# Adaptive layer norm, 32-head attention and a gated feed-forward on one core: earlier weight parts, a wider choice of score bank, and other thresholds for VectorE's share of the softmax

## The chip, the cores and the metric

The kernel runs on one core of a Trainium2 chip. The metric is the device time of one execution in microseconds (us); the median of several executions is quoted. The first execution of the kernel before took 3633 us and is left out of every ratio. A profiled span is some 1.7 us shorter than the time of the same execution.

## The reference

`x` has 2048 tokens of width 512. There are 32 heads of 16, and the feed-forward is 1792 wide. All inputs are bfloat16.

```python
mod = (silu(c) @ w_mod).reshape(1, 6, 1, -1)          # sa, ca, ga, sb, cb, gb
h = layernorm(x) * (1 + ca) + sa
q, k, v = split_heads(h @ wqkv)                       # 32 heads of 16
p = softmax(q @ k.T / 4)                              # 32 x 2048 x 2048 probabilities
x = x + ga * (merge_heads(p @ v) @ wo)
h = layernorm(x) * (1 + cb) + sb
x = x + gb * ((gelu(h @ w_gate) * (h @ w_up)) @ w_down)
```

The 134 million exponentials of the softmax are the bulk of the elementwise work.

## The kernel before

The program is written by a scheduler that runs when the kernel is built. A recorder keeps, for each engine, a model of when it will be free, and a greedy loop picks the next instruction. What the chip gets are fixed streams, one for each engine, run in their order (the 1.22 us wait of VectorE at 742 us in after, below, shows it), with semaphore waits between them. So a constant that looks like a threshold changes the order of thousands of instructions.

Scores are made by TensorE in banks of 128 keys by 512 columns in PSUM. Two engines turn a bank into probabilities:

- ScalarE takes two or three banks in one exponential (1024 or 1536 columns).
- VectorE makes an approximate exponential for the four head positions of one round, a *quad*. It converts each of the four banks to 16-bit integers whose bits are a bfloat16 number (one conversion for each bank), and then writes four copies shifted by a constant (the *shift copies*). The product with V and the sum of the softmax are taken over all five versions, which smooths the approximation. A shift copy may also be done by GpSimd.

The constants that matter, and the place where a quad is started:

```python
AHEAD = 24      # a quad must lie at least so far ahead in the sequence of scores
WIDE = 0        # VectorE's bank may be the last bank of the other half (off)
PRESS = 6       # no new bank for a quad while a waiting quad's unit has so few plain rounds left
QA = 6          # quads only from this round of a unit on (and up to QB)
URGENT = 9      # a shift copy is urgent, and stays off GpSimd, below so many plain rounds
...
if len(mem) == CH and pos >= FIRST and not self.pressed() and self.free["dve"] + 600 < ...:
    while quad is None and cand and rounds[cand[0]][2] < pos + (... AHEAD):
        cand.pop(0)
    ...
self.act(self.E[:, e0:e0 + n, :], self.scp[:, s0:s0 + n, :], ACT.Exp, scale=EXP_SCALE)
...
self.ts("dve", kq[...].bitcast(U16), self.scp[:, gb, :], 128 / OCT, SHIFT_C, ALU.mult, ALU.add)
```

While attention for later tokens runs, the output projection and the feed-forward of earlier tokens are done as *side work* in one PSUM bank, `ps_mi`, and its weights are fetched in parts of 256 KB.

When TensorE would be idle for long, the scheduler puts in *filler* products, whose results nobody reads. They are meant to keep its clock up.

The softmax here doesn't subtract the row's maximum and nothing guards it: scores larger than these inputs give would overflow.

## Time and profile before

| | before |
|---|---|
| median time | 845.5 us (845.4 with one more execution; later sessions 844.6 to 844.9) |
| span of the profiled execution | 842.2 us |
| first attention exponential; end of the last one | 15.5 us; 815.6 us |
| ScalarE idle between these two | 4.2 us |
| score banks on ScalarE / VectorE (counted in the program) | 1704 / 344 |

The head of the profile's page shows the busy time of each engine and its share of the span, and the chain of work that ended last, by engine and by line.

```profile
span 842.2 us, 28224 instructions
PE 780.4 (93%) x12684; PEld 278.9 (33%) x12689; DVE 710.2 (84%) x1345; ACT 810.1 (96%) x747; POOL 117.7 (14%) x71
ACT 79%; PE 12%; DVE 4%; DMA 3%; SPq 1%; issue 0%; DVEq 0%
ACT E L364 76%; PE ps_mi L351 5%; PE ps_sc L351 5%; ACT wreg L364 3%; PE ps_pv L351 2%; DMA rb<-scr_rec 1%; DMA scr_rec<-rden 1%; SPq L415 1%; DVE mreg L376 1%; DVE wreg L381 0%; DMA xs<-in_A_x_dram 0%; DMA mreg<-in_B_w_down_dram 0%; DVE st L404 0%; DVE wreg L368 0%; DVE dreg L376 0%
```

ScalarE is busy for 96% of the span, and three quarters of the chain are its exponentials. TensorE is busy for 93% too, but part of that is filler.

These are the groups of instructions by form on ScalarE. The columns are: line, engine, operation, tiles and shapes, count | busy us, mean ns of one | idle us before it and what ended most of that.

```profile
L364 ACT ACTIVATE E<-ps_sc 128x1536 bf16<-128x1536 f32 x320 | 453.7, 1538 | 3.1 <-PE ps_sc L351 2.8
L364 ACT ACTIVATE E<-ps_sc 128x1024 bf16<-128x1024 f32 x372 | 366.0, 1133 | 1.5 <-PE ps_sc L351 1.4
```

And the largest groups of VectorE's conversions and of the shift copies on VectorE and GpSimd (the others write or read the tile `mreg`; in all there are 344 conversions, and 284 + 60 copies):

```profile
L376 DVE TENSOR_SCALAR dreg<-ps_sc 128x512 uint16<-128x512 f32 x228 | 153.9, 685 | 21.3 <-PE ps_sc L351 19.6
L376 DVE TENSOR_SCALAR mreg<-dreg 128x2048 uint16<-128x2048 uint16 x185 | 119.6, 683 | 3.1 <-PE ps_pv L351 2.8
L376 POOL TENSOR_SCALAR mreg<-dreg 128x2048 uint16<-128x2048 uint16 x43 | 81.5, 1898 | 309.3 <-DVE mreg L376 92.3
```

A mean times a count is more than the busy time on ScalarE (1538 ns x 320 is 492 us), because the instructions overlap. What one exponential costs in a full queue is its spacing. In a row of three 1536-wide ones (4.13 us in all, where a lone one took 1.45 us), that is (4.13 - 1.45) / 2 = 1.34 us.

Busy time by windows, with the columns busy us (and count) for PE, PEld, DVE, ACT and POOL, then the granted TensorE clock, the DMA share and GB/s:

```profile
117.00:640.00 523.00, 492.41 (x6910) 149.56 (x6911) 481.59 (x844) 521.54 (x484) 108.02 (x57) 1.00 0.14 39
640.00:806.00 166.00, 150.49 (x3335) 66.83 (x3332) 107.34 (x216) 164.60 (x137) 0.00 (x0) 1.00 0.38 108
```

In the 523 us of the middle ScalarE is busy for 521.5 and VectorE for 481.6. VectorE has real room in the last stage only, where it is busy for 107 of 166 us.

### The profile page before, as it was taken

What the parts mean: (1) busy time and instruction counts of PE and PEld (TensorE: products, weight loads), DVE (VectorE), ACT (ScalarE), POOL (GpSimd) and SP (SyncE); (2) the same over time, 40 slices, a digit from 0 to 9 for tenths busy, and PEclk for the clock granted to TensorE, in tenths of its full rate; (3) what the DMA queues carried; (4) which work ended last, traced back from release to release, by engine and by line L of the source; (5) the groups of instructions that cost most, each with busy time, mean ns of one, the idle gap of its engine ahead of it and who ended that gap; (6) DMA issues with size and microseconds to landing.
All of it is one profiled execution on the core that took longest, in us unless ns stands there. A gap on an engine that the chain in (4) does not pass through costs nothing.

```text
span 842.2 us, 28224 instructions
## 1 busy us (share of the span) xinstructions
PE 780.4 (93%) x12684; PEld 278.9 (33%) x12689; DVE 710.2 (84%) x1345; ACT 810.1 (96%) x747; POOL 117.7 (14%) x71
## 2 busy tenths in 40 slices
PE   8899999999999998989999999899998998988997
PEld 3333333322222222222222222222343333335556
DVE  7878899899899999999889999999887886376484
ACT  5999999999999999999999999999999999999982
POOL 1000102031220331142210130333000000000000
PEclk9999999999999999999999999999999999999999
DMA  9000000000003111111003111111013222185330
GB/s 315 13 27 17 16 15 15 17 15 15 15 16 90 44 36 52 52 41 46 16 28 96 52 53 32 48 40 40 27 25 103 78 72 65 37 235 158 92 96 14
DMA packets 74931, 47.68 MB, mean 57 GB/s; under 512 B 17693, under 2 KB 70618, under 8 KB 74810
## 3 DMA queue, kind: packets, MB, share of 16 engines
q1 hardware_dynamic: 72426, 44.30, 18.1%
q8 instruction: 99, 1.62, 0.8%
q10 hardware_dynamic: 2384, 1.57, 0.7%
q14 instruction: 22, 0.18, 0.1%
HBM read 43.25 MB, written 2.61 MB: 54 GB/s over the span
## 4 chain that ended last, share of the span: by engine, by line
ACT 79%; PE 12%; DVE 4%; DMA 3%; SPq 1%; issue 0%; DVEq 0%
ACT E L364 76%; PE ps_mi L351 5%; PE ps_sc L351 5%; ACT wreg L364 3%; PE ps_pv L351 2%; DMA rb<-scr_rec 1%; DMA scr_rec<-rden 1%; SPq L415 1%; DVE mreg L376 1%; DVE wreg L381 0%; DMA xs<-in_A_x_dram 0%; DMA mreg<-in_B_w_down_dram 0%; DVE st L404 0%; DVE wreg L368 0%; DVE dreg L376 0%
## 5 line engine op out<-in xcount | busy, mean ns | idle before, releaser
L364 ACT ACTIVATE E<-ps_sc 128x1024 bf16<-128x1024 f32 (+2 forms) x700 | 782.7, 1311 | 17.4 <-PE ps_sc L351 16.9
L351 PE MATMUL ps_sc<-qT,kmo 32*128 32x512 bf16 (+2 forms) x1408 | 171.9, 323 | 10.5 <-ACT E L364 9.3
L351 PE MATMUL ps_sc<-qT,kme 32*128 32x512 bf16 (+2 forms) x1344 | 162.1, 331 | 18.2 <-ACT E L364 16.5
L376 DVE TENSOR_SCALAR dreg<-ps_sc 128x512 uint16<-128x512 f32 x228 | 153.9, 685 | 21.3 <-PE ps_sc L351 19.6
L351 PE MATMUL ps_pv<-E,vaug 128*17 128x512 bf16 (+2 forms) x2308 | 157.1, 321 | 1.3 <-DVE vaug L385 0.8
L351 PE MATMUL ps_pv<-mreg,vaug 128*17 128x512 bf16 (+2 forms) x1644 | 129.1, 354 | 4.1 <-DVE mreg L376 3.1
L376 POOL TENSOR_SCALAR mreg<-dreg 128x2048 uint16<-128x2048 uint16 x43 | 81.5, 1898 | 309.3 <-DVE mreg L376 92.3
L351 PE MATMUL ps_mi<-wreg,mreg 128*32 128x512 bf16 (+1 forms) x1792 | 113.7, 355 | 10.2 <-DVE wreg L381 5.5
L376 DVE TENSOR_SCALAR mreg<-dreg 128x2048 uint16<-128x2048 uint16 x185 | 119.6, 683 | 3.1 <-PE ps_pv L351 2.8
L351 PEld LDWEIGHTS ps_sc<-qT,kme 32*128 32x128 bf16 x1344 | 42.8, 91 | 146.5 <-ACT E L364 123.0
L376 DVE TENSOR_SCALAR mreg<-ps_sc 128x512 uint16<-128x512 f32 x116 | 78.5, 685 | 14.9 <-PE ps_sc L351 13.8
L351 PEld LDWEIGHTS ps_sc<-qT,kmo 32*128 32x128 bf16 x1408 | 46.4, 91 | 128.0 <-ACT E L364 101.7
L351 PEld LDWEIGHTS ps_pv<-E,vaug 128*17 128x17 bf16 x2308 | 47.6, 89 | 62.9 <-issue 50.8
L376 DVE TENSOR_SCALAR mreg<-mreg 128x2048 uint16<-128x2048 uint16 x99 | 65.1, 686 | 3.0 <-PE ps_pv L351 2.5
L351 PEld LDWEIGHTS ps_mi<-wreg,mreg 128*32 128x32 bf16 x1792 | 39.4, 95 | 57.4 <-issue 18.9
L351 PEld LDWEIGHTS ps_pv<-mreg,vaug 128*17 128x17 bf16 x1644 | 37.5, 88 | 51.0 <-DVE mreg L376 24.5
L385 DVE CAST wreg<-ps_mi 128x512 bf16<-128x512 f32 x49 | 33.6, 687 | 15.9 <-PE ps_mi L351 15.6
L376 POOL TENSOR_SCALAR mreg<-mreg 128x2048 uint16<-128x2048 uint16 x17 | 32.3, 1897 | 93.8 <-DVE onorm L368 23.0
L381 DVE SCALAR_TENSOR_TENSOR wreg<-wreg,ps_mi 128x512 bf16<-128x512 bf16 x49 | 33.4, 682 | 12.8 <-PE ps_mi L351 5.6
L351 PE MATMUL ps_mi<-hreg,wreg 128*32 128x512 bf16 x480 | 39.5, 384 | 0.5 <-DVE qT L376 0.5
L351 PE MATMUL ps_mi<-wo,onorm 128*32 128x512 bf16 x480 | 36.6, 382 | 0.1
L368 DVE TENSOR_TENSOR wreg<-wreg 128x1024 bf16<-128x1024 bf16 (+1 forms) x56 | 34.1, 618 | 0.5
(138 smaller groups left out, 597.8 us busy)
## 6 DMA issues: line engine op xcount, KB each, us to landing
mreg<-in_B_w_up_dram SPq DMA_DIRECT2D x32, 256.0 KB, 3.1
mreg<-in_B_w_gate_dram SPq DMA_DIRECT2D x28, 256.0 KB, 2.9
rb<-scr_rec SPq DMA_DIRECT2D x96, 64.0 KB, 2.0
mreg<-in_B_w_down_dram SPq DMA_DIRECT2D x16, 256.0 KB, 2.8
dreg<-in_B_w_down_dram SPq DMA_DIRECT2D x12, 256.0 KB, 4.0
mreg<-in_w_mod_dram SPq DMA_DIRECT2D x1, 2048.0 KB, 14.4
out_dram<-xs SPq DMA_DIRECT2D x16, 128.0 KB, 1.8
rb<-scr_rec SPq DMA_DIRECT2D x52, 32.0 KB, 2.6
```

The source lines that it names most:

```text
L351: return self.rec("pe", lambda e: e.matmul(out, lhsT, rhs, start=start, stop=stop, tile_position=tp), [lhsT, rhs], [out], cost=(n, int(rhs ...
L364: return self.rec("act", lambda e: e.activation(out, in_, func, scale=scale, **kw), rd, wr, cost=self.cost("act", out, [in_], "act"))
L368: return self.rec(eng, lambda e: e.tensor_tensor(out, a, b, op), [a, b], [out], cost=self.cost(eng, out, [a, b], "tt"))
L376: return self.rec(eng, lambda e: e.tensor_scalar(out, a, s1, s2, **kw), rd, [out], cost=self.cost(eng, out, [a], "ts"))
L381: return self.rec("dve", lambda e: e.scalar_tensor_tensor(out, a, s, b, op0=op0, op1=op1), rd, [out], cost=self.cost("dve", out, [a, b], " ...
L385: return self.rec(eng, lambda e: e.tensor_copy(out, in_), [in_], [out], cost=self.cost(eng, out, [in_], "ts"))
L415: return e.dma_start(out, in_)
```

## The change

Its intent in a few words: weight parts of the feed-forward are fetched two chunks ahead; VectorE's score bank may take the free side bank; shift copies turn urgent later, and quads come sooner. The diff, cut to its core:

```diff
-AHEAD = 24
+AHEAD = 20
-WIDE = 0
-PRESS = 6
+SIDE = 1024
+PRESS = 5
-QA = 6
+QA = 5
-URGENT = 9
+URGENT = 6
 ...
         def load(x, ci):
-            if flow and ci < len(chunks):
+            if flow and ci < len(chunks) and not self.dry:
 ...                              (the fetch becomes a task of the SP queue)
-            load(0, 0)
-            load(1, 0)
+            for i in range(2):
+                load(0, i)
+                load(1, i)
 ...                              (G and U: load(x, ci + 1) before the chunk's products becomes)
+                if b0 + kpb >= m:
+                    load(0, ci + 2)          # after them; likewise load(1, ci + 2)
 ...
-                        if n == CH and (s0 or not WIDE or pos < nsplit + 12
-                                        or self.probe(lambda: self.mm(self.scp[:, SC - 1, 0:P], *filler)) > t + 30):
+                        if n == CH and (self.open or self.credit > SIDE
+                                        or self.probe(lambda: self.mm(self.mi[:, 0:P], *filler)) > t + 30):
                             continue
 ...
                     if n == CH:
-                        gb = SC - 1
+                        gb = self.mi[:, :]
```

With the side bank, VectorE's bank needs no place among the score banks, so ScalarE's exponential keeps all three of its banks.

More of the change, by code (lines that the diff above doesn't have):

```diff
@@ L946, in load @@
         def load(x, ci):
-            if flow and ci < len(chunks):
+            if flow and ci < len(chunks) and not self.dry:
                 v = (self.B_w_gate, self.B_w_up)[x].rearrange("(a p) n -> p a n", p=P)
-                self.dma("sp", self.wst[x][ci % 2], v[:, :, 2 * P * ci:2 * P * ci + 2 * P], "st%d%d" % (x, ci % 2))
+                self.task([("sp", lambda: self.dma("sp", self.wst[x][ci % 2], v[:, :, 2 * P * ci:2 * P * ci + 2 * P],
+                                                   "st%d%d" % (x, ci % 2)))], None)
         def load_down(i):
@@ L979, in G @@
             g, w = self.gw[:, ci % 2, 0, 0:m * W], self.gw[:, ci % 2, 1, 0:m * W]
-            load(0, ci + 1)
             for b0 in range(0, m, kpb):
@@ L996, in U @@
             yield from self.until(("gelu", gi, ci))
-            load(1, ci + 1)
             for b0 in range(0, m, kpb):
@@ L1001, in U @@
                 yield from up(1, ci, sub)
+                if b0 + kpb >= m:
+                    load(1, ci + 2)
                 self.stt(w[:, W * b0:W * (b0 + k)], w[:, W * b0:W * (b0 + k)], 1.0, mi[:, 0:W * k], ALU.add, ALU.mult)
@@ L1349, in stream @@
                         mem, after = take(CH)
-                gb = s0 + CH - 1
+                gb = self.scp[:, s0 + CH - 1, :]
                 if g is not None:
                     for n in (CH, CH - 1):
-                        if n == CH and (s0 or not WIDE or pos < nsplit + 12
-                                        or self.probe(lambda: self.mm(self.scp[:, SC - 1, 0:P], *filler)) > t + 30):
+                        if n == CH and (self.open or self.credit > SIDE
+                                        or self.probe(lambda: self.mm(self.mi[:, 0:P], *filler)) > t + 30):
                             continue
@@ L1364, in stream @@
                     g += j
-                items = [(m, s0 + i) for i, m in enumerate(mem)]
+                items = [(m, self.scp[:, s0 + i, :]) for i, m in enumerate(mem)]
                 if g is not None:
@@ L1381, in stream @@
                         pass
-                    self.ts("dve", kq[:, 512 * j:512 * j + 512].bitcast(U16), self.scp[:, gb, :], 128 / OCT, SHIFT_C,
+                    self.ts("dve", kq[:, 512 * j:512 * j + 512].bitcast(U16), gb, 128 / OCT, SHIFT_C,
                             ALU.mult, ALU.add)
@@ L1436, in qk @@
         for kk in range(max(512 // it[0][0][3] for it in items)):
-            for ((_, qd, q0, W), r, j), k in items:
+            for ((_, qd, q0, W), r, j), bank in items:
                 kpb = 512 // W
@@ L1442, in qk @@
                 dc, ee = qd // 2, qd % 2
-                self.mm(self.scp[:, k, W * kk:W * kk + W],
+                self.mm(bank[:, W * kk:W * kk + W],
                         self.km[ee][32 * j:32 * j + 32, dc, P * kt:P * kt + P],
```

## The prediction

> **What bounds the kernel.** Page: span 842.2 us, timed median 845.5. ScalarE is busy 810.1 us, 782.7 of it in softmax exponentials; the chain that ended last is 76% those. Busy time by windows: ScalarE is idle about 15 us before the first exponential, 1.8 in 15:117, 1.5 in 117:660, 1.4 in 660:817 and 19 in the tail after 817. Between 15 and 817 us the time is the number of score banks that ScalarE must exponentiate. VectorE takes the other banks (a 685 ns conversion each, then four 685 ns shift copies per quad of four banks, or 1.9 us each on GpSimd) and is 92% busy in 117:660, 65% in 660:817. TensorE is 93% busy, part of it fillers. Waits on weight transfers: some 3 us on TensorE, none on ScalarE, so fetching two chunks ahead removes little.
>
> **What the change moves** (instructions of both programs, counted in order):
> - VectorE takes 376 score banks instead of 344: 8 more quads. ScalarE: 1536-wide exponentials 320 to 291, 1024-wide 372 to 399, one more 512-wide. The free side bank is used only 5 times; most of the gain is quad timing.
> - Shifts: VectorE 284 to 269, GpSimd 60 to 107 (203 us instead of 114). VectorE net: about +12 us, all after 640 us, where it has room.
> - TensorE: 8 quads add 12 sets of four 512-wide and 40 sets of 256-wide products (at 0.22 and 0.11 us: 7 us); 27 filler sets fewer (6 us). About level.
> - Transfers keep their number.
>
> **Costing.** Instruction durations overlap on ScalarE (1311 ns times 700 is more than the busy time). Solving the busy sum with 427 ns per further bank, an estimate, gives 1.354 us per 1536-wide and 0.93 us per 1024-wide exponential. Saved: 29 x 1.354 - 27 x 0.93 - 0.49 = 13.7 us, nearly all critical: 5 us before 270 us, 3 in the middle, 5 in the last part. [...]the trace's two mean durations differ by 405.
>
> **What leaks.** TensorE has less slack per exponential, so ScalarE gets 1 to 4 us of new waits, mainly in the last part. Prologue and tail stay. [...]in the trace before one VectorE shift took 1155 ns instead of 685. With 107 shifts there, I expect a few more such stalls, 1 us in effect.
>
> **Prediction:** 833.5 us (1.4% faster), 829 to 841 in 8 of 10. Faster by over 2%: 0.13; within 2%: 0.86; slower: 0.01.
>
> **Signs.** Right: ScalarE busy near 796 us and over 98% between 20 and 800 us; GpSimd near 205 us; VectorE near 720; tail about 25 us; weight waits under 3 us. Wrong: ScalarE idle over 6 us in the middle, waiting on score matmuls (TensorE or VectorE became the bound); VectorE shifts often over 1 us[...]; a longer tail because the last feed-forward isn't done.
>
> **What would make it wrong.** The schedule is fixed by a model at build time; if the real machine drifts from it where GpSimd and VectorE interleave twice as densely, in-order queues lose the gain (toward 841). If the earlier weights also remove small stalls, over 2%.

The forecast's sum is 845.5 - 13.7 = 831.8 us, and 1.7 us of leak, out of the 1 to 4 named, make 833.5. The 427 ns had not been taken from a trace, but the traces show it: lone exponentials of 512, 1024 and 1536 columns took 597, 1023 and 1450 ns in before, so 426 and 427 ns a bank. They also show the two costs: the three- and two-bank exponentials are busy for 778.3 us in before (320 and 372 of them) and for 764.1 us in after (291 and 399), and the two sums together give 1.354 and 0.928 us. For the products, 4, 8 and 12 of 512 columns took 0.39, 0.60 and 0.82 us in before (near 341 us), and 8 and 32 of 256 columns 0.40 and 1.06 us in after (near 750 us): 0.22 and 0.11 us for a further set of four.

## More of the kernel before

In the last 100 us the remaining feed-forward weights are made resident, one part for every three positions of the score sequence:

```python
if parts and pos >= loaded and ("ffn", 2 if early else 3) in self.have:
    parts.pop(0)()
    loaded = pos + 3
```

## The result and the profile after

The kernel after takes 834.7 us in the median of four executions (832.6 to 836.2), against 845.4 before. The ratio is 0.9872, with a 95% interval of 0.9846 to 0.9899; a second session gave 834.6 us and 0.9871. Here and below a ratio is the mean time of one kernel's fast runs over that of the other's of the same rounds, so it is not quite the ratio of the medians. By the threshold of 2% this counts as the same, though it is clear of noise.

The head of the page after:

```profile
span 833.0 us, 28525 instructions
PE 779.5 (94%) x12784; PEld 280.8 (34%) x12789; DVE 722.4 (87%) x1362; ACT 797.2 (96%) x746; POOL 206.7 (25%) x118
ACT 77%; PE 12%; DVE 5%; DMA 3%; SPq 1%; issue 1%; POOL 0%; DVEq 0%
ACT E L364 75%; PE ps_sc L351 5%; PE ps_mi L351 5%; ACT wreg L364 2%; PE ps_pv L351 2%; DMA scr_rec<-rden 1%; DMA mreg<-in_w_mod_dram 1%; DMA rb<-scr_rec 1%; DVE wreg L381 1%; SPq L415 1%; DVE dreg L376 1%; POOL mreg L376 0%; DMA den<-scr_den 0%; DVE wreg L385 0%; DVE mreg L376 0%
```

ScalarE lost 13.0 us of busy time. VectorE gained 12 us and GpSimd 89 us, and TensorE's busy time did not change. The groups on ScalarE, then those of VectorE and GpSimd:

```profile
L364 ACT ACTIVATE E<-ps_sc 128x1536 bf16<-128x1536 f32 x291 | 413.4, 1527 | 5.4 <-PE ps_sc L351 5.3
L364 ACT ACTIVATE E<-ps_sc 128x1024 bf16<-128x1024 f32 x399 | 389.5, 1101 | 1.6 <-PE ps_sc L351 1.1
```

```profile
L376 DVE TENSOR_SCALAR dreg<-ps_sc 128x512 uint16<-128x512 f32 x246 | 166.3, 686 | 25.4 <-PE ps_sc L351 22.7
L376 DVE TENSOR_SCALAR mreg<-dreg 128x2048 uint16<-128x2048 uint16 x178 | 115.6, 683 | 1.0 <-PE ps_pv L351 0.9
L376 POOL TENSOR_SCALAR mreg<-dreg 128x2048 uint16<-128x2048 uint16 x70 | 132.8, 1901 | 278.7 <-DVE mreg L376 137.2
```

There are 29 fewer three-bank and 27 more two-bank exponentials. In all, 1672 banks are left to ScalarE before the tail, and 376 go to VectorE. The windows are the same as before:

```profile
117.00:640.00 523.00, 497.19 (x7089) 151.61 (x7087) 481.36 (x841) 522.52 (x488) 178.29 (x94) 1.00 0.15 41
640.00:806.00 166.00, 152.76 (x3544) 71.28 (x3540) 128.61 (x265) 162.02 (x139) 1.90 (x1) 0.99 0.37 105
```

In the middle nothing is lost: ScalarE is busy for 522.5 of 523 us, and VectorE does as much as before, because GpSimd took shift copies over. In the last stage ScalarE is idle for 4 us instead of 1.4.

It helps to cut each profiled span into three parts. *Attention work* is the time from the first exponential to the table load after the last one, less ScalarE's waits in it. The *rest* is everything else: the prologue, those waits and the tail. Before: 795.9 + 46.3. After: 783.0 + 50.0. So the work fell by 12.9 us and 3.7 us came back. Of these 3.7 us, 1.4 are in the prologue (the first exponential at 16.95 instead of 15.53 us; a second profile of the same kernel had 15.70, so this is not a property of the kernel: TensorE's granted clock was 0.50 from 11.7 to 15.1 us in the one execution, and 1.00 in the other and in before), and 2.1 are new waits in the net. After 720 us before has waits of 1.2 us. These are ScalarE's waits after, between 720 and 806 us:

```profile
ACT E L364 <- PE ps_sc L351: 3.9, 4, 1.7
```

And this is that place in the timelines of VectorE, then TensorE, then ScalarE, of the kernel after (start us, duration us, engine, line, operation, tiles, count; in brackets the idle time just before it and what ended it):

```profile
743.26 0.43 DVE L368 TENSOR_TENSOR onorm<-osb,rb 128x256 bf16<-128x256 f32 x1 [1.22 <-DMA rb<-scr_rec]
743.61 0.73 DVE L376 TENSOR_SCALAR hreg<-xs,mv,rstd 128x512 bf16<-128x512 bf16 x2
```

```profile
744.07 0.66 PE L355 MATMUL ps_mi<-ident,hreg 128*128 128x128 bf16 x4 [1.47 <-DVE hreg L376]
744.67 0.39 PE L351 MATMUL ps_sc<-qT,kme 32*128 32x256 bf16 x6
...
746.10 1.04 PE L351 MATMUL ps_sc<-xs,ident 128*32 128x512 bf16 x8
747.07 0.61 PE L351 MATMUL ps_sc<-qT,kme 32*128 32x256 bf16 x6
```

```profile
745.11 1.45 ACT L364 ACTIVATE E<-ps_sc 128x1536 bf16<-128x1536 f32 x1 [0.81 <-PE ps_sc L351]
747.73 2.92 ACT L364 ACTIVATE E<-ps_sc 128x1536 bf16<-128x1536 f32 x2 [1.17 <-PE ps_sc L351]
752.31 2.87 ACT L364 ACTIVATE E<-ps_sc 128x1536 bf16<-128x1536 f32 x2 [1.67 <-PE ps_sc L351]
```

Read it as a chain. At 742 us the next instruction in VectorE's queue is a normalisation that needs `rb`, the reciprocals of the softmax sums, which come back through memory; they land 1.22 us late. Behind it in the queue stands the instruction that makes `hreg`, which needs nothing of that sort. TensorE has a transpose of `hreg` next in its own queue and stands for 1.47 us, and no filler runs in the gap (TensorE is busy for 0.00 us between 742.64 and 744.07 us), because they too stand behind it. Shortly after this gap TensorE gets slow: the same six score products of 256 columns take 0.39 us at 744.67 and 0.61 us at 747.07, as the granted clock is down, to 0.50 from 745.6 to 749.0 us (such a stretch is called a *dip* below). Until 750.9 us it waits another 1.19 us, for a weight part. ScalarE waits three times, for 3.65 us. Only the second of these waits, of 1.17 us, lies in the dip: the first is over before it, and the third begins after it, at the wait for the weight part.

### The profile page after: what moved, and what is told of

Read it like the earlier page. It is cut to its first block, busy times and chain, and to the rows that moved or that the text cites. A ratio compares the mean times of both kernels' runs of the same rounds, so it can differ in the third digit from the quotient of the medians.

```text
span 833.0 us, 28525 instructions
## 1 busy us (share of the span) xinstructions
PE 779.5 (94%) x12784; PEld 280.8 (34%) x12789; DVE 722.4 (87%) x1362; ACT 797.2 (96%) x746; POOL 206.7 (25%) x118
## 4 chain that ended last, share of the span: by engine, by line
ACT 77%; PE 12%; DVE 5%; DMA 3%; SPq 1%; issue 1%; POOL 0%; DVEq 0%
ACT E L364 75%; PE ps_sc L351 5%; PE ps_mi L351 5%; ACT wreg L364 2%; PE ps_pv L351 2%; DMA scr_rec<-rden 1%; DMA mreg<-in_w_mod_dram 1%; DMA rb<-scr_rec 1%; DVE wreg L381 1%; SPq L415 1%; DVE dreg L376 1%; POOL mreg L376 0%; DMA den<-scr_den 0%; DVE wreg L385 0%; DVE mreg L376 0%
## 5 line engine op out<-in xcount | busy, mean ns | idle before, releaser
L364 ACT ACTIVATE E<-ps_sc 128x1024 bf16<-128x1024 f32 (+2 forms) x699 | 769.2, 1272 | 20.6 <-PE ps_sc L351 19.9
L376 POOL TENSOR_SCALAR mreg<-dreg 128x2048 uint16<-128x2048 uint16 x70 | 132.8, 1901 | 278.7 <-DVE mreg L376 137.2
L376 DVE TENSOR_SCALAR dreg<-ps_sc 128x512 uint16<-128x512 f32 x246 | 166.3, 686 | 25.4 <-PE ps_sc L351 22.7
L351 PE MATMUL ps_sc<-qT,kmo 32*128 32x512 bf16 (+2 forms) x1405 | 166.0, 323 | 10.7 <-ACT E L364 9.1
L351 PE MATMUL ps_pv<-mreg,vaug 128*17 128x512 bf16 (+2 forms) x1896 | 140.9, 346 | 2.0 <-DVE mreg L376 1.0
L351 PE MATMUL ps_mi<-wreg,mreg 128*32 128x512 bf16 (+1 forms) x1792 | 116.4, 356 | 10.2 <-DVE wreg L381 4.8
L376 POOL TENSOR_SCALAR mreg<-mreg 128x2048 uint16<-128x2048 uint16 x37 | 70.2, 1901 | 158.5 <-PE ps_sc L351 56.6
L376 DVE TENSOR_SCALAR mreg<-ps_sc 128x512 uint16<-128x512 f32 x125 | 84.9, 687 | 17.0 <-PE ps_sc L351 16.5
L351 PEld LDWEIGHTS ps_pv<-mreg,vaug 128*17 128x17 bf16 x1896 | 43.7, 89 | 49.6 <-DVE mreg L376 17.1
L376 DVE TENSOR_SCALAR mreg<-mreg 128x2048 uint16<-128x2048 uint16 x91 | 59.2, 685 | 0.2
L351 PEld LDWEIGHTS ps_mi<-wreg,mreg 128*32 128x32 bf16 x1792 | 38.8, 95 | 56.8 <-issue 20.3
L351 PE MATMUL ps_mi<-mreg,hreg 128*32 128x512 bf16 x448 | 38.1, 384 | 0.0
```

The lines of the kernel that those rows point to most:

```text
L351: return self.rec("pe", lambda e: e.matmul(out, lhsT, rhs, start=start, stop=stop, tile_position=tp), [lhsT, rhs], [out], cost=(n, int(rhs ...
L364: return self.rec("act", lambda e: e.activation(out, in_, func, scale=scale, **kw), rd, wr, cost=self.cost("act", out, [in_], "act"))
L376: return self.rec(eng, lambda e: e.tensor_scalar(out, a, s1, s2, **kw), rd, [out], cost=self.cost(eng, out, [a], "ts"))
```

## The experiments

Theory 1: the time follows what is left to ScalarE. Its rivals at first were theory 2 (the gain comes from shift copies moved to GpSimd) and theory 3 (it comes from weights that arrive earlier). Later came theory 4 (what is lost again is lost to late transfers in the last 100 us) and theory 5 (TensorE has simply too little time left per exponential there). In each experiment, what the scheduler made of the edit was counted in the built program before the run.

### One part of the change alone

Each starts from the kernel before (the side bank is never used).

load_only: only the weight parts two chunks ahead, with the old constants.

```diff
-            load(0, 0)
-            load(1, 0)
+            for i in range(2):
+                load(0, i)
+                load(1, i)
 ...                              (and the other hunks of load)
```

> The kernel before with only the weight parts fetched two chunks ahead. Counted in the program: VectorE takes 352 score banks (344 before, 376 after), GpSimd 60 shift copies as before. Theory 1 (the time follows what ScalarE has left to exponentiate; estimate 1.354 us per 1536-wide, 0.93 per 1024-wide exponential): 3.4 us less than before, about 842.0 us. Theory 2 (the gain comes from moving shift copies to GpSimd): no gain, about 845.4. Theory 3 (the gain comes from weights that arrive earlier, so TensorE waits less): most of the 10.7 us, 838 or less.

Measured: 848.7 us, ratio 1.0043 (1.0014 to 1.0073). It is slower than before. Theory 3 falls. Theory 1's number is missed by 6.7 us.

urgent_only:

```diff
-URGENT = 9
+URGENT = 6
```

> The kernel before with only URGENT 9 to 6, so that shift copies go to GpSimd more often: 112 of them instead of 60, VectorE 236 instead of 284, but only 348 score banks on VectorE (344 before). Theory 1: 1.7 us less than before, about 843.7 us, although VectorE is relieved of about 30 us of work. Theory 2: most of the gain, about 836 to 838. Theory 3: no gain.

Measured: 848.0 us, ratio 1.0037 (1.0011 to 1.0064). VectorE's busy time fell by 20 us, to 690.3, and GpSimd's rose to 216.3, and nothing was gained. Theory 2 falls. Theory 1's number is missed here too, by 4.3 us.

quads_only:

```diff
-AHEAD = 24
-PRESS = 6
-QA = 6
+AHEAD = 20
+PRESS = 5
+QA = 5
```

> The kernel before with only the quad timing (AHEAD 24 to 20, PRESS 6 to 5, QA 6 to 5): 356 score banks on VectorE, 67 shifts on GpSimd, 289 on VectorE. Theory 1: 5.1 us less than before, about 840.3 us, if VectorE, which now has 12 conversions and 5 shifts more, does not hold anything up. Theory 2 and 3: about 845; a loss, if VectorE at over 90% busy is what limits.

Measured: 847.7 us, ratio 1.0029 (1.0007 to 1.0050). Theory 1's number is missed by 7.3 us here. So theory 1 expected each of the three parts to be faster than before, and each was a little slower.

### The change without one part

no_side: the kernel after, with the side bank out of reach.

```diff
-SIDE = 1024
+SIDE = -1000000
```

> The kernel after without the free side bank (never taken): 356 score banks on VectorE, 105 shifts on GpSimd, weights two chunks ahead. After takes the side bank only 5 times. Theory 1: the other 20 banks that are lost with it count, so 8.6 us slower than after, 840 to 843 us. If only the direct use counted, 5 banks of 0.43 us: 2 us slower, about 837. Theory 2 and 3: about as fast as after, 835 to 837.

Measured: 845.5 us, ratio 1.0002 (0.9979 to 1.0025). The whole gain is gone with a bank that is used five times. Theory 1 named 840 to 843, so it is missed by 2.5 us, but in the right direction. Counting direct uses would have given 837.

old_load: the kernel after, with weight parts one chunk ahead as before.

```diff
-            for i in range(2):
-                load(0, i)
-                load(1, i)
+            load(0, 0)
+            load(1, 0)
 ...                              (and the other hunks of load)
```

> The kernel after with the weight parts fetched one chunk ahead, as before. Counted: 372 score banks on VectorE (376 in after), ScalarE 295 / 395 / 7. Theory 1: 1.7 us slower than after, 836 to 837 us. Theory 3 (earlier weights are what gives the gain): 840 or more. If the two chunks fetched at once crowd the transfers, as theory 4 allows, it could be as fast as after.

Measured: 835.0 us, ratio 0.9887 (0.9873 to 0.9902), 0.15 points behind after, or 1.3 us, in another session. That is about the one quad by which the programs differ, but the intervals overlap.

pool0: the kernel after, without GpSimd.

```diff
-POOLED = 1
+POOLED = 0
```

> The kernel after with no shift copies on GpSimd at all. Counted: the schedule then finds room for only 348 score banks on VectorE (376 in after), 348 shifts on VectorE, ScalarE 321 / 368 / 7. Theory 1: ScalarE's work as in before but for 1.8 us, so 843 to 846 us; GpSimd does not gain time by itself (urgent_only) but is needed to fit the quads. If GpSimd's shifts cost more than they bring[...], it would be below 840.

Measured: 843.2 us, ratio 0.9976 (0.9959 to 0.9993), as theory 1 said. With VectorE alone the scheduler finds room for 348 banks only. GpSimd is needed for the gain, but does not give it by itself.

### How far the other engines are behind ScalarE

narrow480 and narrow480_before: the two kernels with shorter exponentials. The order and number of all instructions stay the same (but for one fill of the columns left out), because the scheduler is still told the old cost.

```diff
-self.act(self.E[:, e0:e0 + n, :], self.scp[:, s0:s0 + n, :], ACT.Exp, scale=EXP_SCALE)
+ew, sw = self.E[:, e0:e0 + n, 0:480], self.scp[:, s0:s0 + n, 0:480]
+self.rec("act", lambda e, ew=ew, sw=sw: e.activation(ew, sw, ACT.Exp, scale=EXP_SCALE), [sw], [ew],
+         cost=self.cost("act", self.E[:, e0:e0 + n, :], [sw], "act"))
 ...
+self.memset(pool, self.E[:, 1:, 480:512], 1.0)
```

> The kernel after with each exponential of a score bank over 480 of its 512 columns; the other columns hold ones, so the result is wrong on purpose. Order and number of all instructions are as in after. ScalarE saves 1671 banks x 32 columns x 0.833 ns = 44.5 us (estimate). If ScalarE alone limits, about 790 us. If the other engines are close behind, as I expect with TensorE at 94% and VectorE at 92% busy, the time falls by 10 to 25 us, to 810 to 825, and ScalarE waits for score products all along: then further quads are worth less and less.

> The kernel before with each exponential of a score bank over 480 of 512 columns (wrong on purpose, order of all instructions as in before). ScalarE saves about 45 us of work (estimate: 1704 banks x 32 columns x 0.833 ns). In after the same cut gave only 9.5 us: there the other engines are that close behind. If the change used up a margin that before still had, this falls by clearly more, 16 to 22 us, to 823 to 829 us, near the same floor as after with the cut. If before had no more margin than after, it falls by about 10, to 835.

The 0.833 ns a column in both is what the traces of before and after show: a lone exponential of 512 columns took 597 ns, one of 1536 columns 1450 ns, and (1450 - 597) / 1024 = 0.833.

Measured: 825.2 us for after with the cut, ratio to before 0.9771 (0.9756 to 0.9786), and 835.1 us for before with the cut, 0.9882 (0.9863 to 0.9900). (Their outputs are wrong, which doesn't matter for the times. The comparison with the reference still passed, so its tolerance does not see this, and these are not valid kernels.) By that cost ScalarE is given 44.5 and 45.4 us less to do, and the time falls by 9.5 and by 9.8 us, just under the 10 to 25 us expected for narrow480. ScalarE's busy time falls by 28.7 and 30.0 us only, because its exponentials overlap less now (a mean of 1379 ns for 1440 columns, where it was 1527 and 1538 ns for 1536; in after, count times mean of the three-bank ones was 31 us above their busy time, with the cut 16 us). The second of the two expectations for narrow480_before holds: no margin was used up. The chain that ended last shows what took over, first in after with the cut, then in before with the cut:

```profile
PE 58%; DVE 25%; ACT 8%; DMA 3%; POOL 2%; issue 2%; SPq 1%; DVEq 0%; POOLq 0%
```

```profile
PE 50%; DVE 28%; ACT 13%; DMA 3%; issue 2%; POOL 2%; SPq 2%; DVEq 0%; POOLq 0%
```

ScalarE's share of the chain is down from 77% to 8%; TensorE and VectorE hold it. So in both kernels ScalarE sets the pace, but in this order of instructions only some 10 us, or 1.2%, ahead of the others. The order was laid out for the longer exponentials; whether one laid out for the shorter ones would be faster was not tried. This floor (the time with the cut) fell with the change, from 835 to 825 us. Which part of the rearrangement lowered it, the runs do not tell: TensorE's busy time is 784.0 and 779.6 us in the two.

### The leak

spread6 and spread5: the kernel after, with the resident weight parts further apart.

```diff
-                    loaded = pos + 3
+                    loaded = pos + 6          # spread5: pos + 5
```

> The kernel after, with the 21 transfers of the last feed-forward's resident weights issued every 6 positions of the score sequence instead of every 3. Counted: exponentials, conversions and shifts are exactly those of after (291 / 399 / 7, 376, 269 + 107); only the order within the last 100 us differs. Theory 4 (the leak of after, 3.9 us of ScalarE waiting between 737 and 754 us, comes from small transfers and weight parts that land late in a crowded transfer queue, and hold up the in-order queues of VectorE and TensorE): these waits go, 831 to 832 us. Theory 5 (TensorE has too little time left per exponential there): no change, 834 to 835.

> The same with every 5 positions. Counted: one more quad on VectorE (380 score banks; ScalarE 287 / 403 / 7). Theory 1: 1.7 us less work for ScalarE than in after, 833.0 us by itself; with theory 4 another 3 us, about 830. Theory 5: the saving is lost to new waits, 834 to 835.

Measured: spread6 832.4 us, ratio 0.9856 (0.9840 to 0.9873). spread5 835.1 us, ratio 0.9894 (0.9878 to 0.9909): one quad more, and slower than spread6. ScalarE's work fell by another 2 us as counted, but the rest grew by 4 (table below); the granted clock was 0.66 in the mean between 800 and 810 us there, where spread6 has 1.00. Theory 4 had named 830 for spread5 and is missed by 5 us; 834 to 835 is what theory 5 had named, so spread5 does not rule theory 5 out. Because the lead of spread6 over after is small, it was repeated with after on one chip:

> The kernel after once more, to compare it with spread6 on one chip: 833 to 836 us.

> spread6 once more beside after on one chip. Theory 4: 1 to 3 us below after. If its lead was the difference of two sessions: equal to after within 0.5 us.

Measured: after 834.6 us (832.9 to 835.9), spread6 832.0 us (830.9 to 834.1), ratios 0.9871 and 0.9844. Spread6 was 2.3 us ahead of after in another session and 2.65 us ahead on the same chip; the intervals of the ratios overlap. It is the fastest kernel, by little. ScalarE's waits in spread6_again between 720 and 806 us, to be held against the 3.9 us above:

```profile
ACT E L364 <- PE ps_sc L351: 1.0, 4, 0.4
ACT wreg L364 <- DVE wreg L368: 0.5, 1, 0.5
```

In this profile most of the leak went. In the first profile of spread6 less of it did: 3.0 us of such waits were left there, 0.9 of them in a dip at 761 us. So spread6 is faster, as theory 4 said, and theory 5, which expected no change of it, does not fit; but the waits went only in part. How they went is less clear still: between 640 and 807 us VectorE still waits for `rb` (5.4 us in four waits, against 3.7 in after_again), and TensorE for a weight part (1.3 us, against 2.5 for two kinds of part). The clock differs too. These are the busy times and the granted clock (third number from the right) of the 20 us around the leak, in before, after, spread6_again, load_only and spread5:

```profile
740.00:760.00 20.00, 16.80 (x334) 6.75 (x326) 12.52 (x35) 20.00 (x18) 0.00 (x0) 1.00 0.82 239
```

```profile
740.00:760.00 20.00, 15.73 (x342) 7.63 (x330) 10.64 (x28) 16.34 (x14) 0.00 (x0) 0.91 0.78 226
```

```profile
740.00:760.00 20.00, 17.33 (x454) 10.32 (x458) 13.34 (x34) 19.22 (x16) 0.00 (x0) 1.00 0.93 272
```

```profile
740.00:760.00 20.00, 15.11 (x306) 6.75 (x294) 9.92 (x31) 17.62 (x15) 0.00 (x0) 0.91 0.89 259
```

```profile
740.00:760.00 20.00, 15.57 (x390) 8.87 (x394) 11.86 (x31) 16.61 (x15) 0.00 (x0) 1.00 0.87 255
```

Transfers fill 78 to 93% of the DMA engines in all five. In before and in spread6_again TensorE's clock stays at 1.00, and ScalarE is busy for 19 to 20 us. In after and load_only the clock falls to a mean of 0.91, and ScalarE is busy for 16.3 and 17.6 us. But in spread5 ScalarE is busy for no more than 16.6 us, and the clock stays at 1.00: TensorE stands for a weight part for 1.71 us and, a little later, for another 2.02 us, and ScalarE once for 2.42 us. So a leak of this size needs no dip. A dip also came in quads_only, where a weight part is awaited at 752 us (timeline of TensorE):

```profile
751.59 0.39 PE L351 MATMUL ps_sc<-qT,kme 32*128 32x256 bf16 x6
753.96 1.90 PE L351 MATMUL ps_mi<-wreg,mreg 128*32 128x256 bf16 x32 [1.98 <-DMA mreg<-in_B_w_gate_dram]
755.79 0.61 PE L351 MATMUL ps_sc<-qT,kme 32*128 32x256 bf16 x6
```

After a gap of 1.98 us, 32 products take 1.90 us (1.06 us at a clock of 1.00, in after at 750.88 us), and six score products 0.61 us instead of 0.39.

### All runs in one table

*Counted* is the change of ScalarE's work against before, from the instruction counts, with 1.354, 0.93 and 0.49 us for a 3-, 2- and 1-bank exponential (0.49 is an estimate: the 597 ns of a lone one less the overlap of 0.11 us, that is 1.45 - 1.34). *Work* and *rest* are read from the profiled execution as defined above, *clock* is the mean granted clock of that execution, and *dips* is the time that its trace shows at a clock of 0.50 before TensorE's last products.

| kernel | banks on VectorE | counted | work | rest | clock | dips | median us |
|---|---|---|---|---|---|---|---|
| before | 344 | 0 | 795.9 | 46.3 | 1.000 | 0 | 845.5 |
| spread6_again | 376 | -13.7 | 783.2 | 46.0 | 0.999 | 0 | 832.0 |
| pool0 | 348 | -1.9 | 794.5 | 47.3 | 1.000 | 0 | 843.2 |
| spread6 | 376 | -13.7 | 783.7 | 47.6 | 0.998 | 3.4 | 832.4 |
| old_load | 372 | -12.0 | 785.4 | 48.2 | 0.998 | 3.4 | 835.0 |
| urgent_only | 348 | -1.7 | 796.0 | 48.8 | 0.996 | 6.8 | 848.0 |
| after | 376 | -13.7 | 783.0 | 50.0 | 0.996 | 6.8 | 834.7 |
| after_again | 376 | -13.7 | 783.2 | 50.1 | 0.997 | 3.4 | 834.6 |
| no_side | 356 | -5.1 | 791.9 | 50.9 | 0.992 | 13.7 | 845.5 |
| spread5 | 380 | -15.4 | 781.5 | 51.7 | 0.996 | 6.8 | 835.1 |
| quads_only | 356 | -5.1 | 791.0 | 55.4 | 0.994 | 10.2 | 847.7 |
| load_only | 352 | -3.4 | 793.0 | 56.8 | 0.990 | 17.1 | 848.7 |

The work follows the counts within 2 us in every row. This checks the counting and the two costs; it is ScalarE's own work laid end to end, so it could not show that ScalarE sets the time. That it does is shown by its waits, 4 to 12 us of the 787 to 805 us from its first exponential to its last. What broke theory 1's numbers for the time is the rest: it runs from 46 to 57 us, and from kernel to kernel it goes with the dips. In quads_only 4.3 of the 9.1 us more than in before are in the tail, with a dip at 819 us in it, and in load_only and spread5 the tail is 2.2 us longer, again with dips. Within one kernel the picture is mixed: the four executions of load_only had clocks of 0.990, 0.992, 0.995 and 0.998 and took 851.52, 850.50, 846.89 and 846.95 us, but those of after all had 0.996 and took from 832.6 to 836.2 us.

So theory 1 holds for the work, and has to be completed for the time: work plus rest, where the rest is larger in the kernels whose in-order queues stand for late transfers in the last 100 us and whose clock dips. (Dips came earlier too: at 12 us in after and no_side, and at 648 us in urgent_only.) That a gap causes the dip, and the dip part of the loss, is read from the timelines and from the table and is not shown. The nearest to it are two profiles of one program: after has the dip at 12 us and begins its exponentials 1.25 us later than after_again, which has none there. No run changed the clock alone, and spread6 also moved some fillers and side products in the last 100 us.

## Why the prediction was right

- The total: 833.5 us predicted, 834.7 measured, inside the range of 829 to 841.
- ScalarE sets the pace. Right: the work fell by 12.9 and 12.7 us in two profiles, where 13.7 were counted; ScalarE's busy time is 797.2 us, 796 predicted; GpSimd's 206.7, predicted 205; VectorE's 722.4, predicted 720.
- "Prologue and tail stay." The tail did (26.6 and 26.7 us). The prologue took 1.4 us longer in one profile of after, where the clock dipped in it, and 0.2 in the other.
- The leak of 1 to 4 us, mainly in the last part. The size was right: 3.7 us, of which 1.4 are the prologue. The reason, "TensorE has less slack per exponential", is not what the trace shows: VectorE and TensorE stood for transfers in their in-order queues between 742 and 751 us, and the clock dipped. And a change in the spacing of weight fetches took the waits after 720 us down from 3.9 and 5.2 us (two profiles of after) to 3.0 and 1.5 us (two of spread6), with as many exponentials, conversions and shift copies.
- That the leak stayed within 1 to 4 us was in part luck. Counted in the same way, with no leak added, the three parts alone were to take 842.0, 843.7 and 840.3 us, and they took 4 to 7 us more; the whole took 2.9 us more than its count of 831.8 us. Nothing in the prediction tells why the whole should leak less than its parts.
- "The free side bank is used only 5 times; most of the gain is quad timing." This was wrong. Without the side bank the gain is nil (845.5 us); with the quad timing alone it is nil too (847.7 us). (After without the quad timing, and before with the side bank alone, were not run.) How often a thing is used directly does not say what a greedy schedule owes to it: with those five places went 20 of the 32 extra banks.
- "Fetching two chunks ahead removes little." Right: taken back, it costs 1.3 us with overlapping intervals; alone, it made the kernel 0.4% slower.
- Stalls of shift copies on VectorE beside those on GpSimd: a few were expected, and after has none. The longest shift copy on VectorE took 696 ns (1155 ns once in before). The reason is in the program: the scheduler's model (`port_at` in the kernel) lets neither engine start such a copy while the other is at one, and in after no copy on VectorE begins more than 0.14 us before the end of one on GpSimd. Where the two met all the same, stalls came: seven in urgent_only, of 2.6 us in all (last section).
- Not foreseen was how close the others are: 10 us behind ScalarE, before and after. The change lowered their floor, as the cut exponentials show it, by 10 us as well; had it stayed at 835 us, after, at 834.7 us, would have had no margin left. The prediction had not costed that floor.

## What to carry to other kernels

Where one engine sets the pace, count what its instruction stream gains or loses in the built program: that predicted the change of its work within 2 us in nine builds. The time also has a part that the counts do not show. Measure how far the next engines are behind (make the pacing instructions shorter without changing the order), and look for places where an in-order queue stands for a transfer: in after TensorE stood for 1.47 us at 742.6 us, and from 745.6 us its clock was 0.50 for 3.41 us (in spread5 it stood for 1.71 us and the clock stayed at 1.00). Parts of a change to a greedy schedule do not add up: here three of the four parts, each alone, lost 0.3 to 0.4% (the side bank alone was not run), and together the change won 1.3%.

## What the traces show of the clock, the overlap, the shift copies and the transfers

- The clock of TensorE: every dip in these traces is at a clock of 0.50 and lasts 3.41 us or twice that, and those of quads_only begin 13.65 and 51.20 us apart, 4 and 15 times 3.41. Dips followed gaps of 1.47 us (after, 742.6 us) and 1.98 us (quads_only, 752 us), with TensorE busy for 1.67 and 1.43 us of the 3.41 us before the dip. No line between dip and no dip comes out of these runs: urgent_only dipped after 2.24 us of busy time (744.04 to 747.45 us), and spread5 did not after 1.71 us and a gap of 1.71 us (750.97 to 754.38 us).
- The overlap on ScalarE: a lone exponential of 1536 columns took 1.45 us, and the spacing of 1.34 us is an overlap of 0.11 us. Durations in a full queue look longer: the mean was 1538 ns before and 1527 after, so count times mean overstates the busy time.
- Shift copies on VectorE and GpSimd: when one on VectorE began well before the end of one on GpSimd, it ended 544 to 548 ns after that end, however long the wait: in all twelve cases over 760 ns (seven in urgent_only, two in no_side, one each in before, load_only and narrow480_before). In before it began at 314.48 us, 0.61 us before the end of the one on GpSimd, took 1155 ns and ended 546 ns after that end; the others took 628 to 696 ns in before and after. What makes VectorE wait is not shown. The copies on GpSimd were never longer than 1902 ns, and VectorE's conversions from PSUM ran beside them at no more than 693 ns (131 in before, 218 in after). This is one of the twelve, in urgent_only, VectorE first:

```profile
416.21 1.30 DVE L376 TENSOR_SCALAR mreg<-dreg 128x2048 uint16<-128x2048 uint16 x1
415.07 1.90 POOL L376 TENSOR_SCALAR mreg<-dreg 128x2048 uint16<-128x2048 uint16 x1 [1.98 <-PE ps_pv L351]
```

- Transfers: in the crowded stretch of after, 735 to 765 us, the 4 KB transfers of the softmax sums, issued by SyncE, had medians of 3.1 and 4.6 us to landing (two of each), and `rb`, of 32 KB, which VectorE stood for, had 3.2 us. In before, 735 to 770 us, they were about as late (3.9, 2.9 and 4.0 us), so lateness alone does not make the leak.
